# Two-part stores, a square root on ACT, early unread products and another instruction order in a one-core delta-rule and MoE kernel

## The chip, the cores and the metric

The kernel runs on one core of a Trainium2 chip. A core has a matrix engine (TensorE, PE in the profile, with PEld for its weight loads), a vector engine (VectorE, DVE), an activation engine (ScalarE, ACT), a general engine (GpSimd, POOL), a queue engine that here only issues transfers (SyncE, SP), and 16 DMA engines that move data between the memory of the chip (DRAM) and the core's buffer. Matrix products land in PSUM, of which the kernel uses eight banks, and are copied from there by DVE or ACT. The engines run side by side, each through its own list of instructions in order, and wait for each other by semaphores.

The metric is the device time of one execution, in microseconds.

## The reference

Two stages. The first is a recurrence over 768 steps for each of 4 batches and 8 heads, with a 48 by 48 state; the second a two-layer network over all 3,072 tokens (4 x 768) of 384 features.

```python
k_n = k / (np.linalg.norm(k, axis=-1, keepdims=True) + 1e-06)
for t in range(S):
    readout = np.einsum('bhd,bhde->bhe', q[:, :, t], state)
    y[:, :, t] = g[:, :, t] * readout
    v_old = np.einsum('bhde,bhd->bhe', state, kt)
    state = state + bt[:, :, :, None] * np.einsum('bhd,bhe->bhde', kt, vt - v_old)

h = x @ w_in                                        # (3072, 384) x (384, 2048)
g = np.maximum(h, 0.0) + np.log1p(np.exp(-np.abs(h)))   # softplus
return g @ w_out                                    # (3072, 2048) x (2048, 384)
```

The result is 3,072 rows of 384 float32. Products are taken in float16 with float32 sums.

## The kernel before, in words

**Chunks and pairs.** The 768 steps are cut into 12 chunks of 64. Inside a chunk the recurrence is solved as a triangular system, so that only the state passes from chunk to chunk. Two chunks are a *pair*, and what doesn't depend on the state is done per pair, for all 32 (batch, head) units and both chunks: `norms`, `front`, `inverse`.

- `norms` (lines 493 to 530): the keys' squares (`ksq`, ACT, line 498), their sums (`red`, DVE, line 502), the square root. The root is `sqrt` on ACT (line 514) for the pairs that `ON_ACT` names, here only pair 0, and a power of 0.5 on POOL (`pow`, line 519) for the five others. Then `eps` on DVE adds a small constant and, but for pair 0, takes the reciprocal (lines 523 and 525).
- `front`: casts of q, products of k with the reciprocal norms (`kmul`, line 323), transposes on PE (`trs`, lines 341 and 384) and their copies (`kev`), Gram products (`gram`, line 456; `gramd`, line 428, for pair 0), their copies (`kkc`) and masks (`mask`, line 471).
- `inverse`: the diagonal blocks go through a transpose on DVE (`ln`, line 564) into a row-by-row solve in 15 steps (`step`, lines 592 and 599), on DVE for pair 0 and on POOL for pairs 1 to 5. It ends with two scalings (`cv`, tile tv, line 224), a cast (`c16`, tile tw) and DVE transposes (`tn`, line 620; `t32`, line 639). From these PE builds the inverse with small products (`xmm`, line 660; `tmm`, line 685; `zmm`, lines 708 and 711). `kd0` and `kd1` prepare the solve's input.

**The chain.** `chain(c)` takes the state through chunk c: products of keys and queries with the state (`ks`, `qs`, line 749), the difference to v (`w`, line 783), the solve by the inverse (`umm`, lines 792 and 796; `zu`, line 817), the new state (`smm`, line 837; `s`, line 852), the outputs (`ymm`, line 867), their product with the gate (`y`, line 882, tile yg) and their transpose (`ytr`, line 901; `xt`). In pair 0, v is first multiplied by the norms (`vs`, line 759).

**The dense part.** `dense(cs)` works on one chunk (0, 1, 10, 11) or two: first-layer products (`g1`, line 931, three of 512 or six of 256 columns), softplus on ACT (`soft`, line 943), second-layer products (`g2`, line 958, four blocks of four products for 128 output rows, all in the one PSUM bank of ring `o`), a copy (`o`, tile osb, three buffers) and a store (line 977). The 128 rows of a copy are 64 rows of one batch and 64 of another, which lie far apart in the result; the store writes them with one transfer. Before the first softplus a small activation (`table`, line 992) loads softplus's table; it depends on the last root that runs on ACT.

**The order.** All of this is a list of 1,197 items. Each has a number, the engines that may run it and the items that it depends on. The string `_ORDER` gives the order in which they are issued, and the engine of each by a letter (P for PE, D for DVE, A for ACT, G for POOL, S for SP). An engine works through its items in that order; buffers are handed out in it too, so a load can also wait for the last reader of its buffer. Keys, values and gates have three buffers each, queries two. All loads of q, k, v and g (94 of 96) and all stores go through SP's queue; the eight weight loads are issued by POOL (line 293).

Of the kernel before, what the change touches and what calls it, by code (L numbers as in the profile page):

```python
# [74 lines left out]
def kernel(  # L75
# [11 lines left out]
    nc = tc.nc  # L87
    B, H, S, D = q.shape
    P = 128
# [7 lines left out]
    ON_ACT = (0,)  # L97
    IDLE = 0
# [819 lines left out]
    def dense(cs):  # L918
# [29 lines left out]
        for c in cs:  # L948
            for p in range(2):
# [24 lines left out]
                def store(en, ob=ob, c=c, p=p):  # L974
                    r0 = p * S + c * C
                    dst = out[r0 : r0 + C, :]
                    nc.sync.dma_start(
                        out=bass.AP(dst.tensor, dst.offset, [(2 * S * DM, 2), (DM, C), (1, DM)]),
                        in_=ob.ap,
                    )  # L980

                add("store", f"{c}.{p}", "S", store, deps=[m3], bufs=[ob])
# [16 lines left out]
    for x in range(IDLE // 6):  # L999
        wb = Buf(p_o)  # L1000
        for y in range(6):

            def fill(en, wb=wb):
                for i in range(8):
                    nc.tensor.matmul(
                        wb.ap[:, 128 * (i % 4) : 128 * (i % 4) + 128], ident, ident
                    )

            add("warm", f"{x}.{y}", "P", fill, bufs=[wb], mm=8, mode="full")
# [4 lines left out]
D166 S8 A9 D138 S0 A1 S25 D137 S24 P141 P139 A106 D107 D110 A142 S3 S2 D111 S10 P151 D152 A140  # L1014
P148 A104 P114 D105 A150 A153 P112 D113 P121 A149 A108 D109 D164 D167 A115 A203 D204 A122 A123
P124 A125 A126 D165 D168 D169 D170 D171 D172 D173 D174 D175 S13 S11 D176 D177 D178 D179 D180
D181 D182 D183 D184 A116 A117 A576 P118 A119 A144 A120 P127 D131 A143 P145 A147 A146 A128 G242
P154 D156 G97 A155 A157 A130 D158 S18 S19 G210 P211 A212 S17 S16 A201 D202 G185 S27 P159 A160
D186 D129 P132 A135 D136 D163 A133 A162 P189 A190 G187 P192 A193 D188 P191 A195 S6 D134 P194
A196 S5 S4 D577 A583 D578 G205 D206 D223 P197 A198 P579 P584 A585 D161 P199 A200 P586 A587 D580  # L1020
P581 S26 S7 A582 S12 D600 G226 P594 P592 S42 P589 S43 D301 P588 D595 S33 S32 A276 D593 P596 S35
A597 S41 S40 D277 D591 D590 G207 P598 S34 A599 P208 P865 D209 A278 D279 P213 D216 D217 A866 A214
D215 P224 A225 P218 P227 D220 A219 D285 P608 A228 P601 G243 A221 G317 D222 G96 P861 A862 G98
D609 D602 P234 A237 A235 D238 P229 D230 P603 S15 A232 A239 P867 P604 D231 D233 P863 A605 D236
A864 P302 P611 A612 A868 D240 G99 P871 A872 S48 P610 P613 G280 P606 A607 D241 A614 D281 D282
A303 P869 P619 P283 P286 A287 P621 D298 A870 P299 D284 P293 S14 D622 D620 P623 D624 A300 A294
P875 A876 P873 A874 D295 P288 D290 D292 A291 D289 P304 D308 D307 D306 P895 A896 P903 A904 P309
D311 D297 S49 A351 D352 P899 A900 P901 A310 A902 G100 P877 S57 D313 P897 P615 P616 D617 S56 A353
A898 G101 P878 P889 A312 A296 A890 P893 A894 D618 P625 P632 G102 A305 G103 P879 P880 G244 G245
G246 G247 G248 G249 G250 G251 G252 G253 G254 G255 G256 G257 G258 G259 G260 S51 A314 D354 D261  # L1030
D262 P268 G263 D264 A881 A269 P265 P891 A266 S50 D360 P361 P270 P267 A271 P883 P884 S20 P627
D315 A362 D316 S21 D633 D626 G355 D356 D357 P272 A273 P635 A636 P628 D629 P274 D275 S64 P885
P886 D887 P634 S59 P637 D638 A892 P630 P358 S65 A426 A631 D427 P645 P639 P640 A359 P905 S22 S23
D646 D642 P368 D641 D369 D370 S58 A376 G318 D372 G319 G320 G321 P906 G322 G323 G324 P377 G325
G326 A371 G373 A378 P907 P643 P363 A366 A364 P649 D644 S28 S29 D650 S73 G392 P656 D657 P908 A909
D367 G327 G328 G329 P374 A375 P647 D648 P659 A660 P652 D653 D365 P911 P384 D388 D387 D386 S72
A428 D429 P658 P661 A662 P912 P651 P654 A385 A655 P669 P913 S30 S31 D670 P667 D668 P379 S74 S75
A451 P664 P663 D665 A382 A380 P671 P914 D672 P452 A453 P941 S37 A942 S36 P919 A920 G330 G331
G332 G333 G334 G335 G336 D337 P343 D666 P673 P925 P947 A344 A948 S67 D383 A926 P680 D381 G338
D339 P345 S38 G393 G389 D390 D391 S89 G430 D681 P340 A341 P931 P943 A932 A944 S66 S882 P342 S88  # L1040
P923 A915 D346 A924 D431 D674 D432 P937 P683 A684 P349 D350 A938 P347 D348 D435 P676 A677 P921
A922 P933 A934 S46 P433 P675 P678 P682 A503 D434 P685 A686 P927 A679 A928 P929 A930 P436 D504
A437 S39 S44 P693 D694 S916 S77 S888 P687 P688 P691 D690 G394 G395 G396 G397 G398 G399 G400 G401
G402 S45 D692 S54 G448 G403 P939 A940 D689 P945 A946 P443 A444 P438 A439 P695 D445 P917 S90 S80
S81 D696 A918 P449 A450 S53 D440 D442 P935 A936 A446 P949 D441 S910 P697 D698 P704 D705 D447
P454 A457 D458 S91 A501 P950 P951 P459 D463 P707 D456 A455 A462 G404 P700 G405 G406 A708 D701
P952 S82 A953 D461 D502 A460 P706 P709 A710 G407 G408 G409 G410 G411 D412 G413 P699 P702 A703
A464 D465 P955 P956 P957 P958 A959 S83 S47 P717 D718 P418 P712 D466 P715 G505 D716 P711 P415
A416 D414 P961 P962 A510 D714 D419 P719 A720 P963 P964 A965 P981 A982 P999 A1000 D713 P728 P417
S55 S86 D506 P420 P723 P721 S954 S52 D729 D421 A526 P730 D722 P527 A528 S60 G523 P524 P1001 S960  # L1050
P511 A525 P967 A1002 G542 S68 D467 D507 P968 P731 D512 A732 P424 D425 S62 P422 A423 G468 P724
G469 P983 G470 G471 G472 G473 G474 G475 G476 G477 D725 G478 A984 P534 A537 D538 P726 P985 A986
D536 D535 P508 D509 P969 P970 D971 A727 P739 D740 P529 D533 D531 P733 A734 P997 A998 P518 A519
P741 D742 P995 D520 P973 D532 A996 A974 A530 D522 G479 G480 G481 G482 G483 G484 P743 D744 D521
P975 P977 P735 P736 D738 D737 P513 D515 D517 S61 A976 P987 A978 A516 A988 P991 A992 A514 P745
P752 P747 P989 A990 P1003 A1004 D746 P748 A749 D753 P755 A756 P979 A980 G485 S79 G486 D487 P490
A491 S972 G539 D540 P754 P757 A758 P750 D541 P993 A994 G488 D489 P1005 P1006 D751 P1007 P1008
A1009 P765 P763 G543 G544 S63 D766 P760 D764 P759 P492 D762 P493 P767 A494 D768 S76 S1010 D761
P1011 P1012 P1013 P1014 A1015 P495 D496 P776 S69 D777 P769 D770 P1047 A1048 P1017 P1018 P1019
P1020 D1021 P779 D780 P497 P772 A773 P499 P1043 P1031 P1023 A1044 A1032 D498 P1024 P1033 A1034  # L1060
P771 A500 S93 P778 P781 D782 G545 G546 S71 G547 G548 S70 S1022 S85 S966 G549 G550 G551 G552 G553
G554 G555 G556 G557 G558 G559 G560 G561 D562 P774 A775 P1059 A1060 P1045 A1046 P789 D790 P784
# [46 lines left out]
```

## Time and profile before

| | us |
|---|---|
| median of three runs | 276.32 (274.16, 276.49, 276.32) |
| the profiled execution | 274.83 |
| its span, first to last instruction | 273.1 |
| PE busy | 226.6 (83%) |
| DVE, ACT, POOL busy | 147.4, 146.1, 135.5 |
| first dense product starts | 42.93 |
| last product ends | 260.42 |
| second pair's solve on POOL starts | 54.35 |
| mean granted clock of PE | 0.974 |

The profile comes from one execution. A busy PE is not PE at its peak: matmuls are pipelined, and their ends are modelled. In lines of instructions, the columns are start, duration, engine, line of the kernel, operation, output and inputs with their tile names, count, and in brackets the idle time before it with what ended that. In the page's slices each digit is the busy share of one fortieth of the span, in tenths. In the chain of work that ended last each piece is what the end waited for at that time. SPq stands for SP's queue.

### The profile page before, as it was taken

To read this page: it belongs to the slowest core of one execution; us is meant where nothing else is said; L and a number is where in the kernel's file an instruction comes from. 1 tells how busy PE (TensorE), PEld (TensorE's weight loads), DVE (VectorE), ACT (ScalarE), POOL (GpSimd) and SP (SyncE) were. 2 spreads that over 40 slices of the span, in tenths; PEclk is the share of its full clock that TensorE was granted. 3 is DMA by queue.
4 is the path that set the end of the run, shared out by engine and by line. 5 is a ranking of instruction groups with operands and counts; after the bars stand their busy time and mean duration, and the time that the engine had idled before them with its cause. 6 is when DMAs were issued, how large, how long until landed. Compare 5 with 4: busy or idle time off the path is not lost.

```text
span 273.1 us, 11156 instructions
## 1 busy us (share of the span) xinstructions
PE 226.6 (83%) x4976; PEld 155.3 (57%) x4976; DVE 147.4 (54%) x304; ACT 146.1 (54%) x277; POOL 135.5 (50%) x229
## 2 busy tenths in 40 slices
PE   0443589999699899997999999999979999999910
PEld 0332477777566566654676567666635566777500
DVE  8697788877767787574766765365121042210000
ACT  3682666888556657846565662356414672363200
POOL 8312796888988899889168898820000000000000
PEclk9999999999999999997999999999979999999995
DMA  8999849999949751487542403521310310110111
GB/s 118 204 201 180 124 99 179 191 205 179 180 77 183 158 112 38 102 129 172 116 92 37 105 15 84 103 75 38 93 30 8 96 46 32 36 53 16 42 50 40
DMA packets 85472, 27.56 MB, mean 101 GB/s; under 512 B 75568, under 2 KB 85424, under 8 KB 85424
## 3 DMA queue, kind: packets, MB, share of 16 engines
q1 hardware_dynamic: 79376, 23.21, 44.7%
q0 software_dynamic: 3968, 3.25, 7.6%
q10 hardware_dynamic: 2080, 0.39, 1.1%
q8 instruction: 39, 0.64, 1.0%
q14 instruction: 9, 0.07, 0.1%
HBM read 25.26 MB, written 4.72 MB: 110 GB/s over the span
## 4 chain that ended last, share of the span: by engine, by line
PE 50%; POOL 14%; DVE 12%; DMA 11%; issue 5%; ACT 2%; SPq 1%; DVEq 0%; ACTq 0%; POOLq 0%
PE o L958 17%; PE h L931 15%; DMA kf<-in_k_dram 5%; POOL tmp L592 4%; POOL tt L599 4%; DMA gf<-in_g_dram 3%; PE d L749 3%; DMA out_dram<-osb 2%; POOL nv L519 2%; PE d L341 2%; PE d L867 2%; DVE tt L599 2%; PE d L817 2%; PE d L901 1%; PE d L685 1%
## 5 line engine op out<-in xcount | busy, mean ns | idle before, releaser
L943 ACT ACTIVATE ga<-h 128x512 f16<-128x512 f32 x96 | 56.8, 597 | 33.0 <-PE h L931 29.5
L931 PE MATMUL h<-xt,w_in 128*128 128x512 f16 (+1 forms) x384 | 73.2, 329 | 0.4 <-ACT ga L943 0.4
L958 PE MATMUL o<-w_out,ga 128*128 128x384 f16 x384 | 72.9, 336 | 0.6 <-ACT osb L214 0.6
L958 PEld LDWEIGHTS <-ga 128*128 128x128 f16 x384 | 36.7, 101 | 25.5 <-issue 4.4
L931 PEld LDWEIGHTS <-w_in 128*128 128x128 f16 x384 | 35.0, 99 | 19.6 <-issue 0.4
L599 POOL TENSOR_TENSOR tt<-tt,tmp 128x30 f32<-128x30 f32 (+7 forms) x75 | 28.4, 379 | 5.9
L592 POOL TENSOR_TENSOR tmp<-nn,tt 128x30 f32<-128x30 f32 (+7 forms) x75 | 27.2, 362 | 5.7
L519 POOL TENSOR_TENSOR nv<-nv,half_c 128x32 f32<-128x32 f32 x5 | 27.3, 5469 | 4.5 <-DVE nv L502 4.5
L214 ACT ACTIVATE kqt<-d 128x1024 f16<-128x1024 f16 (+1 forms) x22 | 19.2, 886 | 5.8 <-PE d L384 4.5
L882 DVE TENSOR_TENSOR yg<-d,gf 128x384 f16<-128x384 f32 x24 | 12.7, 550 | 17.2 <-DMA gf<-in_g_dram 9.6
L783 DVE TENSOR_TENSOR w<-vf,d 128x384 f16<-128x384 f32 x22 | 11.3, 544 | 19.6 <-PE d L749 15.6
L471 DVE TENSOR_TENSOR mt<-d,mask 128x256 f16<-128x256 f32 x48 | 18.6, 416 | 5.7 <-ACT kk L214 3.4
L214 ACT ACTIVATE u<-d 128x384 f16<-128x384 f32 x33 | 15.7, 489 | 10.8 <-PE d L817 5.7
L214 ACT ACTIVATE osb<-o 128x384 f32<-128x384 f32 x17 | 8.3, 490 | 23.8 <-PE o L958 21.4
L214 ACT ACTIVATE kk<-d 128x256 f16<-128x256 f32 x38 | 13.5, 387 | 13.3 <-DVE mt L471 10.7
L456 PE MATMUL d<-kqt 48*64 48x128 f16 x384 | 12.6, 242 | 9.4 <-ACT kk L214 4.5
L749 PE MATMUL d<-s,kqt 48*64 48x48 f16 x704 | 15.8, 188 | 2.8 <-ACT kk L214 2.1
L749 PEld LDWEIGHTS <-kqt 48*64 48x64 f16 x704 | 13.0, 108 | 8.8 <-issue 8.6
L216 DVE CAST u<-d 128x384 f16<-128x384 f32 x15 | 8.2, 553 | 18.2 <-PE d L817 14.4
L456 PEld LDWEIGHTS <-kqt 48*64 48x64 f16 x384 | 8.4, 118 | 14.4 <-issue 13.6
L341 PE MATMUL d<-ident,kn 128*128 128x128 f16 x96 | 9.1, 250 | 6.7 <-DVE kn L216 6.5
L498 ACT ACTIVATE ksq<-kf 128x768 f32<-128x768 f32 x12 | 10.1, 843 | 8.3 <-DMA kf<-in_k_dram 8.1
(102 smaller groups left out, 358.3 us busy)
## 6 DMA issues: line engine op xcount, KB each, us to landing
qf<-in_q_dram SPq DMA_DIRECT2D x24, 192.0 KB
vf<-in_v_dram SPq DMA_DIRECT2D x24, 192.0 KB
gf<-in_g_dram SPq DMA_DIRECT2D x24, 192.0 KB
out_dram<-osb SPq DMA_DIRECT2D x24, 192.0 KB
kf<-in_k_dram SPq DMA_DIRECT2D x22, 192.0 KB
w_in<-in_moe_w_in_dram POOLq DMA_DIRECT2D x4, 384.0 KB, 7.0
w_out<-in_moe_w_out_dram POOLq DMA_DIRECT2D x4, 384.0 KB, 7.8
kf<-in_k_dram ACTq DMA_DIRECT2D x2, 192.0 KB
```

What stands on the lines that cost most here:

```text
L214: nc.scalar.activation(o, x, AF.Copy, scale=float(sign))
L341: nc.tensor.transpose(o[:, p, i], kx.ap[:, p, 2 * i : 2 * i + 2].rearrange("p h d -> p (h d)"), ident,)
L456: nc.tensor.matmul(o[HALF[r], i], x[:, :C], x)
L471: nc.vector.tensor_tensor(mt[c][m].ap[:, NP * p : NP * p + NP], gb[m].ap.rearrange("p (n b) -> p n b", n=NP)[:, :, C:], mask[:, None, :].b ...
L519: lambda en: nc.gpsimd.tensor_tensor(nv.ap, nv.ap, half_c, ALU.pow),
L592: eng.tensor_tensor(t, nn.ap[:, :, j + 1 :, j : j + 1].broadcast_to([P, 2, n, w]), tt.ap[:, :, j : j + 1, :w].broadcast_to([P, 2, n, w]), ...
L599: eng.tensor_tensor(rows, rows, t, ALU.add)
L749: nc.tensor.matmul(hd(o.ap)[HALF[r], NP * p + i], kq_of(c)[FEAT[m], 8 * p + 2 * i + r, off : off + C], s0[r].ap[FEAT[m], NP * p + i], **st ...
L882: lambda en, m=m: nc.vector.tensor_tensor(heads(yg.ap, m), hd(yp[m].ap), heads(gf.ap, m), ALU.mult),
L931: nc.tensor.matmul(hp.ap[:, n * b : n * b + n], w_in[:, j, f * P : (f + 1) * P], xt.ap[:, j, t0 : t0 + n], start=(j == 0), stop=(j == 2),)
L943: lambda en, hp=hp, o=gb: nc.scalar.activation(o.ap, hp.ap, AF.Softplus),
L958: nc.tensor.matmul(op.ap[:, :DM], b.ap[:, col + c0 : col + c0 + 128], w_out[:, f, :], start=(f == 0), stop=(f == NF - 1),)
```

## The change

1. **Stores.** The one transfer of 2 x 64 rows becomes two of 64 rows, one for each half of the buffer's partitions: 48 stores in place of 24.
2. **Root.** `ON_ACT` names pairs 0 and 1, so pair 1's root is a square root on ACT. The item `table` then depends on it.
3. **Unread products.** `IDLE` goes from 0 to 24. 24 new items of three products each, identity with four copies of the identity side by side (512 columns), go into the PSUM bank of ring `o`. Nothing reads them.
4. **Order.** `_ORDER` is another one throughout, with 1,245 items. Items from the first store on have new numbers.

```diff
     RAW = (0,)
-    ON_ACT = (0,)
-    IDLE = 0
+    ON_ACT = (0, 1)
+    IDLE = 24
...
-                def store(en, ob=ob, c=c, p=p):
-                    r0 = p * S + c * C
-                    dst = out[r0 : r0 + C, :]
-                    nc.sync.dma_start(
-                        out=bass.AP(dst.tensor, dst.offset, [(2 * S * DM, 2), (DM, C), (1, DM)]),
-                        in_=ob.ap,
-                    )
-
-                add("store", f"{c}.{p}", "S", store, deps=[m3], bufs=[ob])
+                for r in range(2):
+
+                    def store(en, ob=ob, c=c, p=p, r=r):
+                        r0 = (2 * r + p) * S + c * C
+                        nc.sync.dma_start(out=out[r0 : r0 + C, :], in_=ob.ap[HALF[r]])
+
+                    add("store", f"{c}.{p}{r}", "S", store, deps=[m3], bufs=[ob])
...
-    for x in range(IDLE // 6):
+    for x in range(IDLE // 4):
         wb = Buf(p_o)
-        for y in range(6):
+        for y in range(4):
 
             def fill(en, wb=wb):
-                for i in range(8):
+                for i in range(3):
                     nc.tensor.matmul(
-                        wb.ap[:, 128 * (i % 4) : 128 * (i % 4) + 128], ident, ident
+                        wb.ap.rearrange("p (a b) -> p a b", a=4),
+                        ident,
+                        ident[:, None, :].broadcast_to([P, 4, P]),
                     )
 
-            add("warm", f"{x}.{y}", "P", fill, bufs=[wb], mm=8, mode="full")
+            add("warm", f"{x}.{y}", "P", fill, bufs=[wb], mm=3, mode="full")
```

What the new order does at the start, decoded from its numbers: on PE, five groups of the unread products (15) stand ahead of the first transposes, and the other 19 stand between the transposes and Gram products of pairs 0 and 1, the last of them behind the second `xmm`. On SP, k of chunks 0 and 1 come first, then q of chunk 0, q of chunk 1 mixed with k of chunk 2, then k of chunk 3 and the other queries. On DVE, eight masks, two sums of squares and pair 1's `eps` stand between the steps of pair 0's solve. On POOL, two casts of queries, `kmul` of chunks 2 and 3, `vs` and both copies of v of chunk 0 come ahead of pair 0's `cv`; three of the four loads of the first layer's weights come after `c16`, and pair 1's solve after these. On ACT, `table` stands after pair 0's first `td2`, ahead of its `z`. PE has pair 1's transposes and Gram products ahead of pair 0's `xmm`, and the first `g1` behind chunk 0's chain.

## The prediction

> **What bounds the kernel now.** I read the page's busy times and slices first, then the busy time by stretch, then the chain that ended last, then the waits of TensorE, ACT and the SP queue.
>
> ```profile
> PE 226.6 (83%) x4976; PEld 155.3 (57%) x4976; DVE 147.4 (54%) x304; ACT 146.1 (54%) x277; POOL 135.5 (50%) x229
> ...
> PE   0443589999699899997999999999979999999910
> ```
>
> TensorE (PE) is the engine that fills the span, except in the first five slices and the last two. So I cut the span at the first dense product (42.93), the last product's end (260.42) and the end of data (272):
>
> ```profile
> 30.68:42.93 12.25, 10.60 (x343) 9.81 (x343) 10.86 (x18) 7.62 (x17) 11.04 (x8) 1.00 0.55 93
> 42.93:260.42 217.49, 206.45 (x4402) 138.38 (x4400) 112.79 (x208) 122.18 (x225) 111.64 (x195) 0.98 0.49 94
> 261.00:272.00 11.00, 0.00 (x0) 0.00 (x0) 0.00 (x0) 0.00 (x1) 0.00 (x0) 0.70 0.13 49
> ```
>
> The columns are length, busy time of PE, PEld, DVE, ACT, POOL, granted clock, share of the 16 DMA engines, GB/s. From 42.93 to 260.42 PE is busy 206.45 of 217.49 us: the middle is PE's work plus 11.04 us of gaps. The third row is the surprise: 11 us in which nothing computes and the stores move at 49 GB/s with a DMA share of 0.13, which is two engines of 16. In time, the end looks so:
>
> ```profile
> 257.66 2.76 PE L958 MATMUL o<-w_out,ga 128*128 128x384 f16 x16 [0.58 <-ACT osb L214]
> 260.51 0.49 ACT L214 ACTIVATE osb<-o 128x384 f32<-128x384 f32 x1 [2.90 <-PE o L958]
> ```
>
> PE ends at 260.42, the last copy at 261.00, the span at 273.1. From the chain, start and middle:
>
> ```profile
> 25.27 1.85 POOL tv L224 x2
> ...
> 29.52 5.48 POOL nv L519
> ...
> 35.02 0.80 DVE nv L523
> ...
> 40.20 1.01 DVE yg L882 x2
> ...
> 42.08 0.85 PE d L341 x8
> 42.93 1.28 PE h L931 x6
> ...
> 47.76 0.76 PE h L931 x6
> ...
> 54.35 1.92 POOL nn L582 x2
> ```
>
> ```profile
> 189.96 9.35 DMA gf<-in_g_dram
> ...
> 201.18 3.43 PE o L958 x12
> ```
>
> The second pair's power on POOL (5.48 us) holds VectorE, and so the first outputs (yg), until 35. Six 256-column products take 1.28 us at 42.93 and 0.76 at 47.76 (0.65 later): PE works at half pace until about 47, though the granted clock reads 1.00 there. After a gap of 1.81 us before 200.48 (a gate load that took 9.35 us) it does so again: 12 products of 384 columns in 3.43 us instead of 1.95, and there the granted clock does fall (0.58 from 200.5 to 204.6). A gap of 2.12 us before 124.32, behind a key load, is followed by 16 in 4.17 instead of 2.60.
>
> **The stores.** A store is 128 rows of 1,536 B, 192 KB, written with an outermost dimension of two; at 49 GB/s it takes 4.0 us, and at 261.00 the queue is nearly three stores behind (11 us). In the change each transfer has 64 outermost rows, as the k, v and g loads have. Such a load of 192 KB, in the stretch from 213.7 to 214.6, moved at 226 GB/s with a share of 1.00. So I take 96 KB at 226 GB/s, 0.43 us. The new tail, from PE's last end: 0.09 to the copy, 0.49 copy, 0.6 for the first issue (two took 1.17 us at 209.06), 1.1 from the second issue to first bytes (issue at 209.06, bytes after 210.1), 0.43 data, 1.3 from the last byte to the end of the span (271.8 to 273.1): 4.0 us instead of 12.7, **8.7 less**. If the halves stay on two engines the gain is nothing; the extra issue then costs 0.6.
>
> The Trainium skill (DMA: Bandwidth & Descriptors, "Why a DMA increments its semaphore by 16 and not by 1") says that a transfer uses the largest number of engines up to 16 that divides the slowest dimension of both sides: two here, 16 after. By that rule, the trace's 0.13 and 1.00 agree. The same page's fixed cost of about 2.0 us per transfer would make the tail some 0.9 us longer than my rows; no run here shows it by itself.
>
> The 24 added issues (0.57 us each, 13.6 us in all) lie on SP, whose queue has long waits for output copies (72 us in all). Loads queue behind stores there. Going through the new order, the tightest such load (v of chunk 11) is used 12 us of PE work after the copy that its queue waits for, so I cost this at nothing; without that cover a late load costs 3.4 us (1.81 gap, 1.5 half pace). Two engines that no longer serve stores for 7.7 us (the pair issued at 186.54) should take that g stall away: **1.81 + 1.5 less**. The 0.58 wait at 257.66 for an output slot goes too.
>
> **The square root.** One POOL instruction of 5.47 us becomes one ACT instruction; the first pair's took 0.23 us. The softplus table load (1.28 us, plus a 0.20 us dummy), at 14.80 now, must follow it and moves into the first chain of chunk 0, ahead of ACT's copy of z. The weight loads that POOL issues (0.8 us each) also move: three stand between the first solve's copies and the second pair's solve.
>
> **The order, up to the first dense product.** The keys of chunks 0 and 1 are now loaded first (before, k3 came between); k0 landed at 9.25 with six transfers issued, so with four I put the first solve's input 1.7 us earlier. But DVE now has, among the steps of that solve, eight masks (0.416 each), two sums (0.947) and the norms' two operations (0.27 + 0.35): 5.8 us. The steps end at 25.2 - 1.7 + 5.8 = 29.3 instead of 25.2; with 1.85 for tv and 1.02 for tn the first xmm comes at 32.2 (30.68 before). POOL has the keys' products, the value scaling and two casts (some 9 us) ahead of tv, from about 21: about the same 30. The chain of chunk 0 then took 12.25 us, which contained DVE's hold by the power; now it has kd1 and ln of the second pair (1.30 + 1.04) and the table load in it: 9 to 12. First dense product: **43**, within 39 to 51 (below), no gain by itself. But by then the second pair's transposes and Gram products are done: with 0.45 per eight transposes, 0.43 per Gram block, 0.67 per dense block and so on for the other groups, PE's work from first dense product to end sums to 218.8 us before and 216.1 after; the first is 9% above what the trace took, so **2.5 less**. The second pair's solve starts once ln is done, at 37 instead of 54.35; with the 15.7 us that it took it ends at 53, just ahead of PE (43 + 9.9 of work + 2 of half pace): the gap of 2.24 us before the second pair's first product goes. Later solves then have 10 to 20 us to spare, so POOL doesn't become the bound.
>
> **The 72 products.** They read the identity and write a buffer not needed until the first output block; no instruction waits for them but PE's own queue. No row shows a product of 512 columns alone; three of them in a dense block took 0.65 us at full pace, and the 1.28 of 42.93 is the nearest for half pace. So 24 groups cost 15.6 us or 30.7. PE has 20.1 us of work before 42.93 now, at half pace throughout, some 5 more of it by then in the new order, 39 us at most with the products at full pace: it fits before 43. I take nothing, and nothing gained either, since the chain of small products after the last group is like that of 30.68 to 42.93, which left PE at half pace.
>
> The Trainium skill (TensorE: Matmul & The Clock Gate, Part 1) says the array runs at half clock until a window of about 3.4 us has been busy, and falls back after an idle one. The step from 1.28 to 0.76 within 4.8 us and the dips after the two gaps agree; the granted clock of 1.00 before 47 does not.
>
> **Sum.** Work 206.45 - 2.5 - 1.5 = 202.4; gaps 11.04 - 1.81 - 2.24 - 0.58 = 6.4; from 43 that ends at 251.8; tail 4.0 gives a span of 255.8. The profiled execution took 274.83 for a span of 273.1, so 1.73 is added: 257.5, **258**. The three runs before lie from 274.16 to 276.49, median 276.32, 1.5 above the profiled one; what measurement can tell from no change is about 1%.
>
> **Rivals.**
> - *The products run at half pace.* 30.7 + 25 of own work from 1.5 on puts the first dense product at 57, not 43: 272. It decides once less than about half of them run at full pace. For it: PE at half pace up to 47 although busy 10.6 of 12.25 us. Against: that work is small; dense products brought the pace up within 4.8 us, and the first 15 stand back to back ahead of the first keys.
> - *Other stalls.* The order is new everywhere, and loads' arrivals can't be read from it. Four more stalls like the key load's (2.12 + 1.57) give 258 + 15 = 273. For it: two such in the old order. Against: engines 0 and 1 are free of stores.
> - *The halves land no faster: slower.* In the new order eight output copies stand only 1.2 to 4.9 us of PE work behind the store that frees their slot (before, one at 1.1, the others from 6.2). The chain shows 6.56 us for a store to land; with that, these eight are short by 30 us together. Half of it covered by other products leaves 15, and the tail's 8.7 is not gained: 282. It decides where landing exceeds about 5.5 us.
> - *Better*: groups that bring PE to full pace early, and fewer gaps: 39 for the start, 4 us fewer gaps: 249.
>
> **Chances.** Forecast 0.65 (250 to 267), half pace 0.11, other stalls 0.11, no faster landing 0.07, better 0.06. Faster by over 1% takes the forecast, the better case and most of the second and third: 0.85; within 1%: 0.08; slower: 0.07. The range of 249 to 272 leaves out the slower case and the worst of the two before it.
>
> **What would show it.** A DMA share near 1 in short bursts where stores run, and about 4 us from PE's last product to the end; nv's power with four instances, an ACT square root of 0.23; no half pace after a g load; first dense product between 40 and 46, second pair's solve from about 37. Wrong would be: first dense product after 50, new PE gaps before output copies, or a tail over 8 us.

## The result and the profile after

The changed kernel takes 263.15 us (median of 258.06, 261.39, 264.92 and 266.35); the kernel before, timed beside it, 275.78. The ratio is 0.943, with an interval of 0.930 to 0.955. Ratios, here and below, leave out executions that took over 1.5% longer than the quickest of their kernel, so the ratio of the medians is another (0.954 here), and both profiled executions of the changed kernel, 264.92 and 267.07 us, are among those left out. The forecast was 258 with a range of 249 to 272. So the sign and the range hold, and the likeliest value is 5 us too low.

The page of the profiled execution (264.92 us), busy times and slices:

```profile
span 263.0 us, 11352 instructions
...
PE 238.1 (91%) x5048; PEld 156.9 (60%) x5048; DVE 154.5 (59%) x319; ACT 143.1 (54%) x269; POOL 126.2 (48%) x222
...
PE   7795296789969999699999999999999999999993
...
PEclk9999859599997999968999999999999999999999
```

The two idle slices at the end have become one. But PE, busier at the start because of the unread products, has holes in the fourth, fifth, seventh and eighth slice (20 to 33 and 39 to 53 us), and the granted clock, which stayed near full before, dips there and at two later places. Cut where the prediction cut it, at the first dense product (51.18), the last product's end (258.87) and the last copy (259.4), by stretches (columns as before):

```profile
0.00:51.18 51.18, 36.68 (x700) 21.45 (x701) 41.05 (x108) 27.69 (x57) 29.04 (x57) 0.87 1.14 171
51.18:258.87 207.69, 201.44 (x4350) 135.42 (x4348) 113.41 (x212) 114.93 (x211) 97.15 (x166) 0.97 0.49 90
259.40:263.00 3.60, 0.00 (x0) 0.00 (x0) 0.00 (x0) 0.00 (x0) 0.00 (x0) 1.00 0.23 55
```

| us | before | forecast | after |
|---|---|---|---|
| start, to the first dense product | 42.93 | 43 | 51.18 |
| middle, to PE's last end | 217.49 | 208.8 | 207.69 |
| of it PE busy, and gaps | 206.45, 11.04 | 202.4, 6.4 | 201.44, 6.25 |
| tail, to the span's end | 12.7 | 4.0 | 4.1 |

The middle and the tail came out within 1.2 us of the sum; the start came 8.2 us later than it said. A first dense product after 50 is what the prediction had named as a sign of being wrong. In the timeline the end now reads:

```profile
256.11 2.76 PE L958 MATMUL o<-w_out,ga 128*128 128x384 f16 x16 [0.58 <-ACT osb L214]
...
258.90 0.49 ACT L214 ACTIVATE osb<-o 128x384 f32<-128x384 f32 x1 [2.85 <-PE o L958]
```

The 0.58 ahead of the last products is still there, the only idle time of PE above 0.03 us from 111.3 to its end; the gap and the half pace at 200 are gone. The experiments ask three things: what the stores brought, what the root and the products brought, and where those 8 us are.

### The profile page after: what moved, and what is told of

It is laid out like the page before. It is cut to its first block, busy times and chain, and to the rows that moved or that the text cites. A ratio compares the mean times of both kernels' runs of the same rounds, so it can differ in the third digit from the quotient of the medians.

```text
span 263.0 us, 11352 instructions
## 1 busy us (share of the span) xinstructions
PE 238.1 (91%) x5048; PEld 156.9 (60%) x5048; DVE 154.5 (59%) x319; ACT 143.1 (54%) x269; POOL 126.2 (48%) x222
## 3 DMA queue, kind: packets, MB, share of 16 engines
q1 hardware_dynamic: 80096, 23.21, 50.2%
## 4 chain that ended last, share of the span: by engine, by line
PE 68%; DVE 11%; POOL 8%; issue 7%; DMA 3%; ACT 2%; DVEq 0%; ACTq 0%; POOLq 0%
PE h L931 22%; PE o L958 21%; PE d L749 3%; DVE tt L599 3%; DMA kf<-in_k_dram 3%; POOL tmp L592 3%; PE d L685 2%; PE d L660 2%; PE d L817 2%; PE d L867 2%; POOL tt L599 2%; POOL nv L519 2%; PE d L837 2%; PE o L1003 2%; PE d L901 2%
## 5 line engine op out<-in xcount | busy, mean ns | idle before, releaser
L943 ACT ACTIVATE ga<-h 128x512 f16<-128x512 f32 x96 | 56.5, 597 | 39.4 <-PE h L931 34.2
L592 POOL TENSOR_TENSOR tmp<-nn,tt 128x30 f32<-128x30 f32 (+7 forms) x75 | 29.7, 395 | 5.8
L519 POOL TENSOR_TENSOR nv<-nv,half_c 128x32 f32<-128x32 f32 x4 | 21.9, 5468 | 10.7 <-DVE nv L502 10.7
L216 DVE CAST u<-d 128x384 f16<-128x384 f32 x19 | 10.3, 553 | 22.6 <-PE d L817 9.4
L1003 PE MATMUL o<-ident 128*128 128x512 f16 x72 | 20.7, 429 | 1.4 <-POOL ident masks.py:199 1.4
L214 ACT ACTIVATE u<-d 128x384 f16<-128x384 f32 x29 | 13.9, 492 | 11.5 <-PE d L817 10.8
L749 PEld LDWEIGHTS <-kqt 48*64 48x64 f16 x704 | 13.4, 108 | 8.2 <-issue 8.1
L214 ACT ACTIVATE kk<-d 128x256 f16<-128x256 f32 x34 | 11.7, 382 | 11.8 <-PE d L456 11.3
L216 DVE COPY osb<-o 128x384 f32<-128x384 f32 x8 | 4.4, 556 | 23.3 <-PE o L958 13.0
L456 PE MATMUL d<-kqt 48*64 48x128 f16 x384 | 10.3, 231 | 4.8 <-DVE mt L471 4.8
L817 PE MATMUL d<-u,z 64*64 64x48 f16 x384 | 11.4, 191 | 3.6 <-issue 3.2
```

What stands on the lines that cost most here:

```text
L214: nc.scalar.activation(o, x, AF.Copy, scale=float(sign))
L216: ENG[en].tensor_copy(o, x)
L519: lambda en: nc.gpsimd.tensor_tensor(nv.ap, nv.ap, half_c, ALU.pow),
L592: eng.tensor_tensor(t, nn.ap[:, :, j + 1 :, j : j + 1].broadcast_to([P, 2, n, w]), tt.ap[:, :, j : j + 1, :w].broadcast_to([P, 2, n, w]), ...
L749: nc.tensor.matmul(hd(o.ap)[HALF[r], NP * p + i], kq_of(c)[FEAT[m], 8 * p + 2 * i + r, off : off + C], s0[r].ap[FEAT[m], NP * p + i], **st ...
L817: nc.tensor.matmul(hd(vp.ap)[HALF[r], pi], z.ap[HALF[r], 2 * pi + m, :], u1.ap[HALF[r], pi],)
```

## Experiments on the stores

All experiments were timed beside the kernel before, whose medians were 274.56 to 274.93. The first one only runs the changed kernel again, as the reference for the others.

> The changed kernel as it is, beside the others. From its first profile: tail from PE's last product to the end of the span 4.1 us, first dense product at 51, PE gaps of 4.82 (near 27), 2.93 (near 44), 2.16 (near 77) and 2.50 us (near 109). If the gaps are set by the order, all four are there again within 0.5 us; if those without a named releaser are chance, they are gone or elsewhere, and the time moves with them. Time 258 to 266.

Measured: 265.62 (261.29 to 267.07), ratio 0.958 [0.947, 0.969]; first dense product at 50.30. The four gaps are there again, with 4.82, 3.28, 1.55 and 2.20 us; the third is 0.6 off. In its two sets the executions of this kernel spread over 8 and 6 us, and those of the old order over 1 to 4. In the profiled one of 267.07 PE stays at a granted clock of 0.50 from 46 to 63, where in the one of 264.92 it is 0.93 from 51.2 to 56; behind the first dense product PE is busy for 204.65 us in it, against 201.44. So differences of 2 or 3 us between variants of the new order are not told apart below.

**One transfer again, in the new order.**

```diff
-    for r in range(2): ... dma_start(out=out[r0 : r0 + C, :], in_=ob.ap[HALF[r]])
+    dma_start(out=bass.AP(dst.tensor, dst.offset, [(2 * S * DM, 2), (DM, C), (1, DM)]), in_=ob.ap)
```

> The changed kernel with the one transfer of 2 x 64 rows per output copy. Theory (two engines serve such a store, 4 us each): tail back to 12 to 13 us, DMA share 0.13 in it, and new PE gaps at the output copies that stand close behind the store that frees their slot, up to 15 us in all: 8 to 24 us over the changed kernel. Rival (what ends late is a fixed cost, and halves merely overlap): tail 4 to 6 us, time within 2 us of the changed kernel.

Measured: 280.73 (278.14 to 281.83), ratio 1.021 [1.013, 1.028]: without the split the change is slower than the kernel before. In the profiled execution the last products, and a stretch behind them, read:

```profile
264.60 2.76 PE L958 MATMUL o<-w_out,ga 128*128 128x384 f16 x16 [0.58 <-ACT osb L214]
```

```profile
267.00:276.40 9.40, 0.36 (x3) 0.00 (x0) 0.00 (x0) 0.49 (x1) 0.00 (x0) 0.69 0.12 43
```

PE ends at 267.36 and the span at 276.4: a tail of 9.0 us, at a share of 0.12 and 43 GB/s, the picture of the kernel before; 12 to 13 us was expected. Against the changed kernel the split is worth 15 us here (280.73 - 265.62). In the profiles most of it lies in the middle: cut as before, it is 219.0 us instead of 207.7, half of that in gaps (11.8 against 6.3) and half in PE's busy time; the tail adds 4.9, and the start is 2.8 shorter.

**The split alone, in the old order.**

```diff
-                    nc.sync.dma_start(out=bass.AP(..., [(2 * S * DM, 2), (DM, C), (1, DM)]), in_=ob.ap)
+                    for r in range(2):
+                        r0 = (2 * r + p) * S + c * C
+                        nc.sync.dma_start(out=out[r0 : r0 + C, :], in_=ob.ap[HALF[r]])
```

> The kernel before with its own order, each store issued as two transfers of 64 rows one behind the other. Theory: tail from 12.7 to 4.0, the gate load behind stores lands without a PE gap near 199 (1.8 gap and 1.5 half pace), the 0.6 wait for an output slot gone or not: 8.7 to 12.6 us faster, ratio 0.954 to 0.968. Rival (the order brought the gain): within 3 us of before.

Measured: **258.63** (258.30 to 259.64), ratio 0.942 [0.937, 0.947]. That is 16.3 us less than the kernel before: this one edit alone brings all that the change brings. Its median is 4.5 and 7.0 us below those of the changed kernel's two sets, its ratio the same as in the first (0.943) and below that of the second (0.958); the quickest execution of the changed kernel, 258.06, is as quick as the quickest here. The stretches of its profiled execution, cut as above:

```profile
0.00:42.26 42.26, 20.14 (x575) 16.98 (x576) 34.55 (x97) 23.49 (x51) 23.88 (x34) 1.00 0.99 156
42.26:252.72 210.46, 205.33 (x4404) 138.56 (x4402) 113.62 (x208) 121.57 (x225) 111.70 (x195) 0.98 0.56 99
253.30:256.90 3.60, 0.00 (x0) 0.00 (x0) 0.00 (x0) 0.00 (x0) 0.00 (x0) 1.00 0.23 55
```

The tail is 252.72 to 256.9, 4.2 us: 8.5 less than before. The middle is 7.0 shorter, of which 5.9 are gaps (11.04 to 5.13) and 1.1 busy time; the start is 0.7 shorter (0.2 of it is the view: the timeline gives 42.72 for the kernel before). The gaps before the product at 124.32 (2.12, behind a key load) and before 200.48 (1.81) are gone, that before the second pair's first product is 1.65 instead of 2.24, and three stops without a releaser (2.08 in all; more on them below) have become one of 0.35. Set beside the profiled execution of the changed kernel, the same cut gives the price of all the rest: start +8.9, middle -2.8, tail -0.1, together +6.1 us of span (263.0 against 256.9).

**Is it the number of transfers or their shape?** Two kernels. The first writes each half as four blocks of 16 rows, in the new order; the second keeps one transfer per store in the old order, but with 64 as the outermost dimension and the two batches inside it.

```diff
-  nc.sync.dma_start(out=out[r0 : r0 + C, :], in_=ob.ap[HALF[r]])
+  nc.sync.dma_start(out=bass.AP(dst.tensor, dst.offset, [(16 * DM, 4), (DM, 16), (1, DM)]), in_=ob.ap[HALF[r]])
```

> The changed kernel with each half store written as 4 x 16 rows instead of 64 rows; same bytes, same 48 transfers. Theory (the outermost count sets how many engines serve a transfer): DMA share 0.25 and about 98 GB/s while one runs, a half takes 1.0 us, the last two overlap in one queue: tail 4.8 to 6.5 us, time 0 to 4 us over the changed kernel. Rival (the gain is from smaller transfers or one contiguous block): share near 1 in bursts, tail 4.1.

Measured: 264.78 (263.00 to 268.99), ratio 0.961 [0.954, 0.968], the tail 4.1 us with bursts at a share of 0.6 to 0.74. The expected four engines were not seen. Nothing in this trace sets its stores apart from those of the changed kernel: SP's queue moves the same 80,096 packets, of the same sizes, and those of the last two halves run from 1.15 to 2.40 us behind the last copy in both. The four blocks adjoin, so they may have been carried as one run of 64 rows; that is an argument and was not tested. This run decides nothing about the shape.

```diff
-  out=bass.AP(dst.tensor, dst.offset, [(2 * S * DM, 2), (DM, C), (1, DM)])
+  out=bass.AP(dst.tensor, dst.offset, [(DM, C), (2 * S * DM, 2), (1, DM)])
```

> The kernel before, its old order, with each store still one transfer, but written with 64 as the outermost dimension and the two sequences inside it (64 x 2 rows of 1,536 B), so that the rows land at other places of the output than the reference's; their number and size are unchanged. Theory (what counts is the outermost count, 64 against 2, not the number of transfers): bursts with a share above 0.5 and over 120 GB/s in the tail, about 4 us from the last copy to the end of the span, no half pace near 200, 257 to 260 us. Rival (what counts is that a transfer is a single contiguous block of 64 rows, or that there are twice as many transfers): share 0.13 and 49 GB/s as before, a tail of 11 us, 273 to 276 us.

Measured: 259.82 (258.27 to 261.16), ratio 0.947 [0.938, 0.956]. In time, one transfer per store is as good as two. It is a probe of the shape and no kernel to use: the source was not turned round with the target, so the rows land at wrong places of the result. The issues of its last 18 us, with the median time from issue to landing (the same view gives 2.2 for the halves of the kernel with split stores):

```profile
out_dram<-osb SPq DMA_DIRECT2D x5, 192.0 KB, 2.2
```

All 192 KB land in 2.2 us, in bursts of up to 345 GB/s. So what counts is the outermost count of 64 instead of 2; neither the number of transfers nor a contiguous block of rows is needed. The packets say it too. SP's queue moves 79,376 packets in the kernel before, 79,712 here, and 80,096 with split stores; the rows are the same, and only the packets of 4 B differ: 2 for each store before, 16 for each here, 16 for each half. If every engine that serves a transfer ends with one such packet, which fits the shares, the four-block stores ran on 16 engines too. By the rule of the Trainium skill that the prediction cited (DMA: Bandwidth & Descriptors, "Why a DMA increments its semaphore by 16 and not by 1"), one transfer with 64 outermost would spread over 16 engines; this run agrees, and the four-block run, for which the same rule, taken on the blocks as written, gives four, does not show four.

## Experiments on the root and the products

**The power back on POOL, in the new order.** `ON_ACT` is `(0,)` again, and item `pow 2` goes from A to G.

> The changed kernel with the second pair's root as the power on POOL again, all else as in the change. Theory (the root's 5.2 us saved are given back, because POOL's products of keys then meet VectorE's solve steps, one of which took 5.25 instead of 0.28 us): POOL starts the products of keys some 5 us later, the 5.25 us step is gone or moves, first xmm within 2 us of 38.6, first dense product 50 to 54, time 0 to 4 us over the changed kernel. Rival (the root is worth its 5 us): first dense product at 56, time 5 us over it.

Measured: 269.49 (267.74 to 272.36), ratio 0.978 [0.971, 0.985]: 4 to 6 us over the changed kernel. The power starts as soon as the second pair's sums are there, and what follows it moves back behind it:

```profile
22.44 5.46 POOL L519 TENSOR_TENSOR nv<-nv,half_c 128x32 f32<-128x32 f32 x1 [13.87 <-DVE nv L502]
...
29.71 5.25 DVE L599 TENSOR_TENSOR tt<-tt,tmp 128x120 f32<-128x120 f32 x1
```

The first dense product comes at 57.56 instead of 50 to 51, so the rival holds; the step of 5.25 us has moved and is not gone. In this order the root's move is worth those 4 to 6 us.

**The root on ACT, in the old order with split stores.** `ON_ACT = (0, 1)`, and the table load behind the second root.

> The kernel before with two-part stores (258.6) and the second pair's square root on ACT, softplus's table load moved right behind it; nothing else. Theory (the power holds the first chain until 35): VectorE's eps at 30 instead of 35, first dense product 1 to 3 us before 42.3, time 255.5 to 258. Rival (the table load and its copies in the first chain cost what the root saves, or the products of keys on POOL hold VectorE): within 1 us of 258.6 or above.

Measured: 259.39 (258.49 to 259.62), ratio 0.943 [0.938, 0.948], against 258.63 without: no difference. First dense product at 43.00 against 42.26. But the forecast that VectorE's `eps` comes at 30 was not put to the test:

```profile
35.90 0.18 DVE L523 TENSOR_SCALAR nv<-nv 128x32 f32<-128x32 f32 x1 [2.41 <-ACT nv L514]
```

The sums that the root needs are done at 29.2, but at this place of the order ACT has eight other instructions to do first, and the root starts at 35.65. With the power, the same `eps` began at 34.55. What the root would bring in the old order ahead of those instructions was not run.

**Without the 72 products.** The 24 items and their three products each are dropped from the list; the buffer that they wrote is not read, so nothing of the result is left out.

> The changed kernel without the 72 unread products, same order otherwise. Prediction's view (they cost and bring nothing): time within 2 us of the changed kernel, first dense product within 1 us of 51. Theory that they matter (PE at full pace before 20): eight transposes take 1.03 instead of 0.62 us up to 25, the first solve's input (13.7) comes 1 us later, first dense product 1 to 2 us later. Theory that they hinder: first xmm up to 3 us earlier than 38.6, since 3 + 6 + 3 products (0.75 to 2.5 us a group at half pace) stand right ahead of it.

Measured: 263.26 (261.64 to 267.43), ratio 0.956 [0.950, 0.963]: no difference from the changed kernel (263.15 and 265.62). The early groups of eight transposes take 0.62 us with the products and 1.03 without, so they do raise PE's pace there, but the first dense product stays where it was, at 50.56. PE is busy with them for 20.7 us. (The views read a granted clock of 1.00 where the trace has no entry for it, which is up to 53.6 in this kernel and up to 47.0 in the kernel before; six products of 256 columns take 1.49 us there and 0.83 later, so that reading says nothing of the pace.)

## Experiments on the start

The trace of the changed kernel shows one step of the first solve on DVE that takes 5.25 us instead of 0.28, beside a run of POOL instructions. Timeline of both engines (start, duration, engine, line):

```profile
22.56 0.93 POOL L216 CAST qn<-qf 128x768 f16<-128x768 f32 x1
22.85 5.25 DVE L599 TENSOR_TENSOR tt<-tt,tmp 128x120 f32<-128x120 f32 x1
23.47 2.90 POOL L323 TENSOR_TENSOR kn<-kf,nv 128x768 f16<-128x768 f32 x2
...
26.33 0.23 POOL L574 COPY tt<-beta_l 128x32 f32<-128x32 f32 x1
26.50 1.46 POOL L759 TENSOR_TENSOR vf<-vf,nv 128x768 f32<-128x768 f32 x1
28.02 1.01 POOL L216 CAST w<-vf 128x384 f16<-128x384 f32 x2
...
34.04 0.19 DVE L599 TENSOR_TENSOR tt<-tt,tmp 128x30 f32<-128x30 f32 x1
```

The step begins during the cast of 22.56 and ends at 28.10, 0.14 us after the scaling of 26.50; the steps end at 34.2, where my sum said 29.3. From there to the first small product the trace has:

```profile
34.33 1.84 POOL L224 TENSOR_SCALAR tv<-tt,own 128x256 f16<-128x256 f32 x2 [5.30 <-DVE tt L599]
36.18 2.47 PE L1003 MATMUL o<-ident 128*128 128x512 f16 x6
36.60 1.03 DVE L620 STREAM_TRANSPOSE tn<-tv 128x512 f32<-128x512 f32 x1
38.58 1.19 PE L660 MATMUL d<-tn,kk 64*64 64x32 f16 x64
```

`tv` is done at 36.17, `tn` starts 0.4 us later behind masks of the second pair and is done at 37.63, and PE comes to the small products another 0.95 us later, behind six unread ones.

The hold is not the same in every execution. With the four-block stores, whose start is that of the changed kernel, one step takes 5.25 us as well. With one transfer per store and with four key buffers (below), whose start is the same too, three instructions of DVE are held instead, each beside one or two of POOL; with four key buffers:

```profile
22.49 1.44 DVE L599 TENSOR_TENSOR tt<-tt,tmp 128x120 f32<-128x120 f32 x1
23.97 1.45 DVE L592 TENSOR_TENSOR tmp<-nn,tt 128x126 f32<-128x126 f32 x1
25.45 1.61 DVE L599 TENSOR_TENSOR tt<-tt,tmp 128x126 f32<-128x126 f32 x1
```

The steps then end at 32.5 to 32.8. The first dense product comes at 50.3 to 51.5 in the three traces with the long hold and at 48.3 and 48.6 in these two. The kernel without products has the short hold too (1.53, 1.44 and 1.61) and still comes to 50.56. So the products may bring some 2 us at the first dense product; that is one trace against two, and the times do not show it.

**POOL freed.** Both `kmul` and `vs` go to DVE and the two casts of v to ACT.

```diff
-  kmul k2: G, kmul k3: G, vs 0: G, w0 0.0: G, w0 0.1: G
+  kmul k2: D, kmul k3: D, vs 0: D, w0 0.0: A, w0 0.1: A
```

> The changed kernel with five items taken off POOL at the same places of the order: kmul of chunks 2 and 3 and vs of chunk 0 run on VectorE (1.03 + 1.03 + 1.18 us), both w0 copies on ACT (0.49 each). Theory (VectorE's step of 5.25 us is held by POOL's instructions, which then run back to back for 5.5 us): the longest step is 0.3 to 0.8 us, steps end at 32.3 instead of 34.2, first xmm 1.5 to 2.5 us before 38.6. Rival (the step waits for something else, or VectorE is the bound there): a step of about 5 us stays, first xmm 3 us later by VectorE's added work. In both the gap of about 3 us inside zu stays at the same product (the 17th), if it belongs to a place in PE's list of instructions.

Measured: 262.58 (262.05 to 262.85), ratio 0.954 [0.949, 0.960]. The same step, and the first small product:

```profile
23.18 0.28 DVE L599 TENSOR_TENSOR tt<-tt,tmp 128x120 f32<-128x120 f32 x1
...
29.85 0.19 DVE L599 TENSOR_TENSOR tt<-tt,tmp 128x30 f32<-128x30 f32 x1
...
36.03 1.03 DVE L620 STREAM_TRANSPOSE tn<-tv 128x512 f32<-128x512 f32 x1
...
37.12 1.06 PE L660 MATMUL d<-tn,kk 64*64 64x32 f16 x56 [1.17 <-DVE tn L620]
```

Without POOL's run the step takes 0.28 and the steps end at 30.0, four microseconds earlier, although one of the moved products of keys (0.95) now stands among them; this shows what held it. But `tn` comes only at 36.03: ahead of it in DVE's list stand the second pair's masks (line 471), which wait for that pair's Gram products, and in this kernel the moved `vs` (0.95). So the hold was not the only thing in front; the first dense product came at 50.04, within the 48.3 to 51.5 of the traces with POOL's run, and the time is the same within the spread.

**Four key buffers.** The SP queue waits up to 18.1 us for a key buffer in the changed kernel.

```diff
-    r_k = ring("kf", 3, [P, 2, H, D], F32)
+    r_k = ring("kf", 4, [P, 2, H, D], F32)
-    r_td = ring("td", 3, [P, U, HC], F16)
+    r_td = ring("td", 2, [P, U, HC], F16)
```

> The changed kernel with four key buffers instead of three (and two buffers instead of three for td, to make room). In it the SP queue stood up to 18.1 us for a key buffer, and the third pair's solve was late by 2.50 us at 111.30 in one execution and not in another. Theory (that wait costs the changed kernel a part of what it loses to the old order with split stores): the wait of 18.1 goes, the gap before the third pair's first product is under 0.5, and the time is 259 to 262 us. Rival (the wait is covered, and the loss lies in the start): the wait goes and the time stays at 262 to 267 us, with the gap after the 607th product at 1.5 to 3.7 us as before.

Measured: 264.86 (260.99 to 266.02), ratio 0.957 [0.945, 0.968]. The long wait is gone (that queue's longest for a `kmul` is 2.7 us) and the time stays, with the first dense product at 48.55: the rival holds. Neither did the gap at the third pair's first product go (2.51 us at 110.33), so the key load was not its cause.

**A stop of PE behind its 607th product.** In the changed kernel PE stands 2.93 us in the middle of a run of 32 products that need nothing new, with no releaser (`issue`):

```profile
47.09 0.62 PE L817 MATMUL d<-u,z 64*64 64x48 f16 x15 [2.93 <-issue]
```

```profile
44.16:47.09 2.93, 0.00 (x0) 0.00 (x1) 0.32 (x1) 0.40 (x1) 2.46 (x7) 0.66 1.21 205
47.09:51.20 4.11, 3.69 (x94) 3.57 (x95) 2.46 (x6) 1.95 (x3) 3.48 (x9) 0.50 1.27 162
```

Behind it PE works at a granted clock of 0.50. The kernel without products has the same stop elsewhere in the program, 72 products later:

```profile
48.76 0.41 PE L837 MATMUL d<-u,kn 64*64 64x48 f16 x7 [2.81 <-issue]
```

Counted from the start, both are the 607th product with its weight load. I counted so every stop of PE over 0.35 us that has no releaser, in all kernels of this study: they lie behind product 607, 735, 863, 991, 1375, 1503, 1759, 2527 or 2783, and each of these is 95 above a multiple of 128. 128 products with their weight loads are 256 instructions. The page's list of queues (packets, MB, share) fits that:

```profile
q8 instruction: 39, 0.64, 1.1%
```

PE has 10,096 instructions in all, which is 39.4 times 256; the queue moved 39 packets of 16.4 KB, 64 B for each of 256 instructions. The traces say when each packet moved, and the k-th fits the place behind product 95 + 128 k: in all 14 traces PE passes no such place sooner than 1.2 us after the end of its packet, and all 36 stops end 1.2 to 1.7 us after it. In the changed kernel the fourth packet moves from 44.70 to 45.66, inside the stop that ends at 47.09. So these stops are PE waiting for its next 256 instructions. That the one behind product 607 comes with the new order has a reason too: PE gets through the 128 products ahead of it in 3.2 to 4.0 us there, and needs 7.1 to 8.0 for its products 480 to 607 in the old order, where it has no stop. All stops of 1.3 us or more have a DMA share of 1.18 to 1.35 in them; those where the share was below 1.1 were 0.35 to 1.3 us long, and most boundaries have no stop. One stop at a share of 1.33 was only 0.70, so the load goes with every long one but does not by itself make it. The packets point the same way: 459 of 518 start no later than 2 us after PE has begun the block before theirs, and all 23 that start over 2.9 us after it had a share above 1.1 in between.

**The weights earlier.** POOL's four loads of the first half of the first layer's weights go ahead of its first cast (`G99 G97 G96 G98` in front of `G226`), to take load away from that place.

> The changed kernel with POOL's four loads of the first half of the MoE weights moved ahead of its first cast (to about 8.5 us, where POOL is idle), instead of one at 21.8 and three from 36.9 us. Before 47.09 TensorE stood 2.93 us for nothing named, after its 607th product, while one 16 KB packet of an instruction queue was on its way (0.96 us in the slice 44 to 45) beside a DMA share of 1.2. Theory (the gap is a block of 256 of TensorE's instructions that arrives late because loads fill the engines): the share at that product falls below 1, the gap there to under 1.5 us, the granted clock of the next ten microseconds stays above 0.9, and the first dense product comes at 46 to 49 instead of 50 to 51; 259 to 263 us. Rival (the gap is a fixed cost of that place in the list, whatever is loaded): 2.4 to 3.7 us there, first dense product at 50 to 52, 262 to 268 us. If the key loads are pushed back by the weights, the first small product (xmm, 38.6) comes later, by up to 3 us, and that is added in both.

Measured: 264.25, 264.80 and 268.27, ratio 0.964 [0.955, 0.974], and a profiled execution of 376.43 in which PE's clock was granted at 0.557 over the whole span. The stop is 0.53 us in it, at a share of 0.03, but at that clock this decides nothing. Hence the same kernel once more:

> The kernel with the early weight loads once more, since the profiled execution of it ran at half the granted clock from end to end and three others took 264.3 to 268.3 us. Theory (a late block of instructions): TensorE's stop behind its 607th product is at most 1.5 us with a DMA share under 1.0 in it, where seven executions with shares of 1.19 to 1.28 showed 1.56 to 3.70; the first dense product then comes at 46 to 49. Rival: 2.4 us or more whatever the share. The time in both: 262 to 267 us, as the three.

Measured: 267.95 (265.92 to 269.69), ratio 0.978 [0.972, 0.985]. The stop is 1.80 us, but the share in it was still 1.22: the loads of q and v had moved into the same place, since the weights held the queries back (the first cast of q at 27.50 instead of 21.00) and with them the whole start (first dense product 54.98). The two theories are not told apart by it. That DMA load makes the packets late, and so the stops long, stays a correlation over the kernels; where the stops lie in the list, and that they end with a packet, is shown.

## Why the prediction was right, and where not

- **Stores: right in kind, undersized.** The tail was forecast at 4.0 and is 4.1; one transfer with 64 outermost does as well as two, so the reason given (engines by the outermost count) holds; the tail has no room for the 0.9 us more that the prediction thought possible. I gave the split 8.7 + 3.3 + 0.6 = 12.6 us; alone it brought 16.3. The missing 3.7 lies mostly in the middle: I took out gaps of 1.81 and 0.58; they fell by 5.9, among them the key load's 2.12 and most of the stops for instructions, and the latter differ between executions of one kernel. The 0.58 did not go: it stands in the old and the new order with split stores, so it was no store that PE waited for there. That the other gaps went because two engines were free of stores is an argument; the runs show only that the split took them away. The 24 added issues cost nothing measurable (one against two issues: 259.82 and 258.63). The rival in which halves land no faster is refuted by the landing times: a median of 3.0 us over the changed kernel and 5.8 at most, where it took 6.56.
- **"The steps end at 29.3; first xmm at 32.2": this step failed**, and the 43 with it. Three terms were missing from the sum, which make up the 6.4 us by which the first `xmm` came late. DVE's step stood 5.0 us behind POOL's run, shown by freeing POOL (end at 30.0, near my 29.3); in the other kind of hold it is some 3.6 (1.44 + 1.45 + 1.61, against 0.28 or 0.29 each). Between the last step and `tn` I put only `tv`; the second pair's masks stand there too, and cost 0.4 here and 3.4 with POOL freed, with which `tn` came hardly earlier. And PE had unread products ahead of the first `xmm` (0.95: `tn` done at 37.6, the product at 38.58). What the hold costs the whole kernel is not shown: the edit that removed it did not make the kernel clearly faster. I had listed POOL's work of some 9 us, but only as a term of POOL's own time.
- **"9 to 12" for the chain of chunk 0**: 12.6 (38.58 to 51.18), of which 2.93 is the stop for instructions; without it the chain is inside the forecast. Before, none of the stops fell in front of the first dense product.
- **Work 2.5 less, gaps 6.4**: the middle's busy time is 201.44 against 202.4 and its gaps are 6.25. That the gaps fit is luck. The one before the second pair's first product is gone as forecast (that pair's solve starts at 41.06, before at 54.35, forecast 37). But the key load's 2.12 and the old stops for instructions, which I had left in, went too, and in their place came two such stops (0.69 and 2.16) and 2.50 before the third pair's first product, which waits for its `tn`. (The 218.8 that I scaled the work from is 6% above 206.45 and not 9%; the 2.5 hardly changes.)
- **The products cost and bring nothing**: right for the time, 263.26 without them. In the start they did both: 0.95 us ahead of the first `xmm`, and a quicker pace, which may be worth 2 us at the first dense product. The rival of half pace fell, as their groups in front of the transposes raised PE's pace.
- **The root "no gain by itself"**: not tested in the old order, where the root was as late as the power (259.39 against 258.63), and wrong as a statement on the new one, where putting the power back costs 4 to 6 us, since there it comes in front of what POOL does for the first solve.
- **Other stalls**: of the rivals this one came true in kind, at another place. It put them at late loads; they were a held step, masks in front and a stop for instructions, all in the start, and beyond it 2.16 us of such a stop and 2.50 behind the third pair's solve.

So the change is one good edit and a new order that adds nothing to it: by the medians the order loses 4.5 to 7 us, by the ratios 0 to 4. Old order and split stores, 258.63 us, has the lowest median of all kernels that were run.

## What to carry to other kernels

Look at the DMA share in the last microseconds before anything else: a store whose outermost dimension is 2 runs on two engines here, at a share of 0.13, and splitting it in two was an edit without a price that could be measured. Turning its dimensions round is worth as much in time, but the source must be turned with them, which was not run. When an order is changed, add up what each engine's list puts ahead of the first critical instruction, and then ask which of these instructions hold another engine: here a row of POOL scalings stretched one DVE step from 0.28 to 5.25 us. And when an engine's part moves to another, see what stands ahead of it in the new list: the root on ACT, in the old order, started 6.5 us after its input was there. Time a change's parts apart, since a good part can carry a bad one.

## What the runs showed of the hardware

- One DVE instruction with two inputs was held through five POOL instructions that followed each other closely, for 5.25 us, in four traces; in three others of the same row three instructions were held one after the other, for 1.44 to 1.61 us each. The Trainium skill (SBUF — State Buffer, Terms) says that DVE and GpSimd share a pair of ports under an exclusive lock held for the full instruction, the loser blocking fully. The traces agree that the loser blocks; in the four with 5.25 us it did not get the ports between one POOL instruction and the next either, in the three others it did. What decides between the two is open.
- PE stops for 0.35 to 3.70 us at fixed places of its instruction list, 128 products apart, at some boundaries, and goes on 1.2 to 1.7 us after the end of a 16.4 KB packet of the instruction queue; the long stops all fall where loads fill the DMA engines. In the changed kernel the first of them falls into the chain to the first dense product, and the granted clock behind it is 0.50. How long the clock then stays low (5 us in one execution, 17 in another, with 3.2 us more of PE's busy time) and how long DVE is held are the two differences between executions that could be seen.
- Near the end, where few loads are left, a half store of 96 KB and a single one of 192 KB (64 outermost) land in the same 2.2 us, the latter in bursts of up to 345 GB/s; over the whole execution the medians are 3.0 and 2.8.
- A transfer with an outermost count of 2 moves 2 packets of 4 B beside its rows, one with 64 moves 16; the DMA share while it runs is 0.12 to 0.13 and 0.6 or more.
